# Splitting the next expert's weights into a second pair of tiles, two jobs ahead

## The chip, the core and the metric

The kernel runs on one core of a Trainium2 chip. The metric is the device time of one execution in microseconds (us); where several runs were timed, their median is given. The core's engines are TensorE (PE in the profile, with its weight loads as PEld), VectorE (DVE), ScalarE (ACT), GpSimd (POOL) and SyncE (SP, which here issues DMAs). Each has its own queue of instructions and waits for the others through semaphores. "PEq", "DVEq" or "ACTq" in a row of the trace is the sequencer of that engine: its branches, register operations and waiting steps.

## The reference, cut to what matters

Two stages follow each other. The first is a recurrence over 768 positions for 4 batches and 8 heads; its output is the list of 3072 tokens with 384 channels that the second takes.

```python
for t in range(S):
    cur = einsum('bhd,bhe->bhde', u * k[t], v[t])
    y[t] = einsum('bhd,bhde->bhe', r[t], state + cur)
    state = w * state + einsum('bhd,bhe->bhde', k[t], v[t])

logits = x @ w_gate + modality_bias[modality_id]
e_idx  = argmax(logits);  gate_w = softmax(logits) at e_idx
for e in range(8):
    h = maximum(x[e_idx == e] @ w1[e], 0)       # 384 -> 1024
    out[e_idx == e] = gate_w * (h @ w2[e])      # 1024 -> 384
```

Each token goes to one expert only. With the inputs timed here, three of the eight experts have tokens: 149, 1354 and 1569. The expert with 1569 comes first, that with 149 last.

## The kernel before, in words

**Tiling.** The recurrence is worked in chunks with matrix products (the first stage, up to about 225 us), during which finished tokens are routed and ten portions of 128 tokens of the first expert are already put through its weights (the "slots"). What is left is cut into **jobs** of 128 tokens of one expert. Job 0 stands ahead of a loop, jobs 1 to 15 are turns of it (`For_i`, L1441). Jobs 0 to 2 belong to the first expert that has tokens, 3 to 13 to the second, 14 and 15 to the third.

**Weights.** w1 and w2 of one expert are 6144 fp32 numbers in each partition, `raw`; the first half of the columns is w1, the second w2. For the products they are scaled by a power of two (`ws`) and split into two fp16 tiles: ScalarE writes `whi`, the rounded value, and VectorE `wlo`, what the rounding left (`split`, L954, in pieces of WQ = 1024 columns, six of them). The scale comes from a norm of each piece, taken on ScalarE (`norm`, L916) and summed and turned into `ws` and its inverse `winv` by `scales`. `wf` is the product of the two inverses and belongs to the output's factor; `undo` (L937) renews it. There is one `raw`, one `whi` and one `wlo`, so the weights of the next expert can be loaded while those in use are in `whi` and `wlo`, but not split.

**A job.** On TensorE: the last products of the job before (`low_terms`, from its `hl`), then `up`: the hidden blocks in three groups of 4, 2 and 2 (`phb`, nine terms a block from `whi` and `wlo`), then `high_terms` of this job (`po`, from `hh`). After each group ScalarE evicts it to `hh` (`relu_high`, L1010) and VectorE writes the remainder to `hl` (`relu_low`, L1015). ScalarE also scales the output row of the job before (`otb`, L966, by `fac`), which GpSimd scatters by an indirect DMA. At the end `take_in` (L1398) copies the next tokens, which have landed in `xn` and `mn`, to `mxT` and `mt`, where the next job's products read them.

**What runs in which job.** A table with a column for each job is worked out on VectorE once the tokens are counted (`jobs`, L862 to L888; TensorE then spreads it, L891). Its row CODE holds a small number with bits, which each turn loads into registers of the engines concerned (`at`, L898). Run-time branches (`tc.If`) on that number decide what a turn does. Below, a branch is called *taken* where its body runs and *passed* where it doesn't:

- `first_half` (L1408), at the end of the last job of an expert: the split of w1 into `whi` and `wlo`, once TensorE is through with the old w1.
- `second_half` (L1413), at the start of the first job of an expert: `undo` and the split of w2, with part of the last piece on GpSimd, after the old w2 has been used by `low_terms`.
- otherwise, in the Else of `second_half`, two inner branches (L1430 and L1432), each with three norms of the weights that were loaded since: the first three in the expert's last job but one, the others in its last.

SyncE loads the weights of the expert after next in the first job of an expert (`next_load`, L1435), as soon as `raw` has been read.

**What sets the order.** The first stage and job 0 are one block whose instructions are put in the order of the code on each engine (`manual_schedule`, closed at L1402), but the branch of `first_half` for job 0 (L1440) stands outside of it, as a whole; so does the loop. Within the loop's body, four engines run in the order of the code. At run time, each engine works through its own queue in order.

Of the kernel before, what the change touches and what calls it, by code (L numbers as in the profile page):

```python
# [18 lines left out]
P = 128  # L19
# [16 lines left out]
GONE = 1000  # L36
NQ = 6
# [19 lines left out]
SP, ACT, AD = (mybir.EngineType.SP,), (mybir.EngineType.Activation,), (mybir.EngineType.Activation, mybir.EngineType.DVE, mybir.EngineType.Pool)  # L57
# [3 lines left out]
class _Kernel:  # L61
# [730 lines left out]
    def jobs(self):  # L792
# [62 lines left out]
        eq = new("eq", [P, 4, E])  # L855
        v.scalar_tensor_tensor(eq, csm.unsqueeze(1).to_broadcast([P, 4, E]), self.line, self.grid, ALU.subtract, ALU.is_equal)
# [5 lines left out]
        f, g = new("jf", [P, 4]), new("jg", [P, 4])  # L862
# [5 lines left out]

        last, now, soon, then = (slice(q, q + 1) for q in range(4))
        a, b = new("ja", [P, 1]), new("jbit", [P, 1])
        v.tensor_scalar(a, f[:, now], -1.0, 1.0, ALU.mult, ALU.add)
        v.scalar_tensor_tensor(b, f[:, last], 2.0, g[:, soon], ALU.add, ALU.mult)
        yield
        v.scalar_tensor_tensor(b, g[:, then], a, b, ALU.mult, ALU.add)
# [67 lines left out]
    def wide(self, q, part=0, parts=1, n=1):  # L944

        sl, sc = self.piece(q, part, parts, n)
        self.nc.scalar.activation(self.whi[:, sl], self.raw[:, sl], AF.Copy, scale=sc)

    def fine(self, q, part=0, parts=1):

        sl, sc = self.piece(q, part, parts)
        self.nc.vector.scalar_tensor_tensor(self.wlo[:, sl], self.raw[:, sl], sc, self.whi[:, sl], ALU.mult, ALU.subtract)  # L952

    def split(self, q, parts=1):  # L954
# [138 lines left out]
    def run(self):  # L1093
# [313 lines left out]
        whole = self.late.tile([P, 768], F32, name="scaled")  # L1407
        def first_half(code):  # L1408
            with tc.If(code > 7):
                for q in range(NQ // 2):  # L1410
                    self.split(q, 2 if q == 0 else 1)

        def second_half(code):  # L1413
            with tc.If(code % 8 > 3) as first:
                self.undo()
                self.split(NQ // 2)

                sl, sc = self.piece(NQ - 1, 0, 1)
                lo, hi = slice(sl.stop - 768, sl.stop), slice(sl.stop - 512, sl.stop)
                nc.gpsimd.tensor_tensor(whole, self.raw[:, lo], sc.to_broadcast([P, 768]), ALU.mult)  # L1420
                nc.gpsimd.tensor_tensor(self.whi[:, hi], self.raw[:, hi], sc.to_broadcast([P, 512]), ALU.mult)
                mid = slice(sl.start - WQ, hi.start)
                nc.scalar.activation(self.whi[:, mid], self.raw[:, mid], AF.Copy, scale=sc)
                self.fine(NQ - 2)
                rest = slice(sl.start, lo.start)
                nc.vector.scalar_tensor_tensor(self.wlo[:, rest], self.raw[:, rest], sc, self.whi[:, rest], ALU.mult, ALU.subtract)
                nc.gpsimd.tensor_tensor(self.wlo[:, lo], whole, self.whi[:, lo], ALU.subtract)
            with first.Else():
                with tc.If(code % 4 > 0):
                    with tc.If(code % 2 > 0):  # L1430
                        norms(*range(NQ // 2))
                    with tc.If(code % 4 > 1):  # L1432
                        norms(*range(NQ // 2, NQ))
# [6 lines left out]
        first_half(self.at(CODE, 0, 15, AD))  # L1440
        with tc.For_i(1, nj, 1, iteration_sync="reg_based") as i, tc.manual_schedule(engines={getattr(mybir.EngineType, e) for e in MS[:4]}):  # L1441
            self.turn(0, self.at(ROW, i, E * CAP, SP, 1), mn, xn)
            code = self.at(CODE, i, 15, AD)
            self.low_terms(po)
            second_half(code)
# [7 lines left out]
            first_half(code)  # L1453
# [45 lines left out]
```

## Time and profile before

| | |
|---|---|
| three timed runs | 368.51, 368.72, 372.12 us; median 368.72 |
| the profiled execution | 372.59 us, of it a span of 370.9 us between its first and last instruction |
| mean granted TensorE clock | 0.962 of full speed |
| busy: TensorE / its weight loads | 339.8 / 270.4 us |
| busy: VectorE / ScalarE / GpSimd | 230.5 / 157.5 / 175.0 us |
| instructions | 14643 |

Rows of the timeline read: start in us from the span's start, length of the stretch, engine, line, operation, output <- inputs, shape of output and input, number of instructions in it, and in brackets how long the engine stood idle just ahead and what released it. Rows of the windows give a stretch of time, its length, and each engine's busy time in it with the number of instructions; then the granted clock, the DMA share and GB/s. A row of one line's instructions on a sequencer gives their count, three lengths in ns, and the first and the last start.

### The profile page before, as it was taken

How to read it: one execution, taken by the hardware profiler on the slowest of the kernel's cores; microseconds unless marked ns; L12 is line 12 of the kernel's file. 1: busy time of each engine (PE TensorE's matmuls, PEld its weight loads, DVE VectorE, ACT ScalarE, POOL GpSimd, SP SyncE). 2: the span in 40 equal slices, each digit the busy share in tenths (PEclk: the TensorE clock that was granted, in tenths of full speed). 3: DMA queues.
4: the chain of work that ended last, by engine and by line, in shares of the span. 5: the costliest groups of instructions: out<-in, count | busy, mean ns of one | idle time of the engine just before them, and what ended most of it. 6: DMA issues, size and time to landing. Idle time of an engine off the chain costs nothing. (4 is left out here: it accounts for less than half of the span.)

```text
span 370.9 us, 14643 instructions
## 1 busy us (share of the span) xinstructions
PE 339.8 (92%) x5314; PEld 270.4 (73%) x5314; DVE 230.5 (62%) x754; ACT 157.5 (42%) x371; POOL 175.0 (47%) x252
## 2 busy tenths in 40 slices
PE   7969999898989999999989599998899999999883
PEld 3658888688777978878867487776677788767661
DVE  6996767679979596679755444339533233323960
ACT  7135647534356455646723122227122222265711
POOL 8974656846985778565241711116111112102821
PEclk9986999989998998999989989999999999999999
DMA  6997796569999998966691412213931211212120
GB/s 158 263 221 217 233 264 175 169 149 171 207 272 172 195 257 208 169 190 164 200 184 31 150 23 51 58 43 86 292 73 43 60 46 43 64 21 64 21 55 4
DMA packets 56091, 50.66 MB, mean 137 GB/s; under 512 B 40936, under 2 KB 49641, under 8 KB 55792
## 3 DMA queue, kind: packets, MB, share of 16 engines
q1 hardware_dynamic: 52848, 40.60, 49.4%
q0 software_dynamic: 3200, 9.47, 7.4%
q8 instruction: 30, 0.49, 0.6%
q14 instruction: 13, 0.11, 0.1%
HBM read 30.55 MB, written 11.63 MB: 114 GB/s over the span
## 5 line engine op out<-in xcount | busy, mean ns | idle before, releaser
L1006 PEld LDWEIGHTS <-whi 128*128 128x128 f16 x1248 | 73.7, 98 | 8.9 <-issue 6.2
L1080 PEld LDWEIGHTS <-hh 128*128 128x128 f16 x416 | 38.4, 98 | 30.7 <-ACT hh L1010 5.5
L1006 PE MATMUL phb<-mxT,whi 128*128 128x128 f16 x720 | 47.7, 219 | 0.2 <-DVE mt L1398 0.2
L1006 PEld LDWEIGHTS <-wlo 128*128 128x128 f16 x624 | 38.9, 100 | 3.1 <-DVE wlo L952 3.1
L1010 ACT ACTIVATE hh<-phb 128x256 f16<-128x256 f32 (+1 forms) x45 | 20.2, 453 | 42.4 <-PE po L1080 16.6
L1006 PE MATMUL phs<-mxT,whi 128*128 128x128 f16 x480 | 32.1, 223 | 5.0 <-issue 5.0
L1015 DVE SCALAR_TENSOR_TENSOR hl<-phb,hh 128x256 f16<-128x256 f32 (+1 forms) x45 | 22.8, 512 | 20.7 <-ACT hh L1010 13.7
L345 POOL TENSOR_TENSOR rc<-ud,powr 128x512 f32<-128x512 f32 (+1 forms) x27 | 32.8, 1221 | 0.9 <-DVE w L150 0.9
L648 POOL DMA_INDIRECT rows<-row,posi x24 | 24.3, 1013 | 17.0 <-issue 9.7
L425 DVE TENSOR_TENSOR at<-psc,mask 128x512 f32<-128x512 f32 x48 | 31.6, 682 | 0.8 <-PE psc L419 0.7
L454 PE MATMUL py<-kv,at 128*64 128x48 f32 x768 | 30.9, 236 | 1.2 <-issue 1.2
L454 PEld LDWEIGHTS py<-kv,at 128*64 128x64 f32 x768 | 29.1, 152 | 2.6 <-issue 1.8
L1085 PEld LDWEIGHTS <-hl 128*128 128x128 f16 x208 | 19.6, 98 | 15.6 <-issue 3.5
L419 PE MATMUL psc<-rc,kc 48*64 48x128 f32 x768 | 28.7, 284 | 2.2 <-issue 1.4
L1006 PE MATMUL phb<-mxT,wlo 128*128 128x128 f16 x360 | 28.0, 219 | 2.6 <-DVE wlo L952 2.6
L362 POOL TENSOR_TENSOR rk<-rc,kc 128x512 f32<-128x512 f32 x14 | 17.8, 1274 | 26.1 <-DVE ebx L299 12.2
L530 ACT ACTIVATE row<-py,sx 128x384 f16<-128x384 f32 x24 | 13.9, 579 | 34.3 <-DVE sx L301 19.7
L1090 DVE TENSOR_SCALAR fac<-mt,wf 128x1 f32<-128x1 f32 x16 | 3.4, 213 | 40.2 <-ACT otb L966 32.2
L1080 PE MATMUL po<-wlo,hh 128*128 128x384 f16 x128 | 26.3, 326 | 2.0 <-DVE wlo L952 2.0
L1080 PE MATMUL po<-whi,hh 128*128 128x384 f16 x128 | 26.8, 327 | 0.6 <-ACT hh L1010 0.6
L975 POOL TENSOR_TENSOR seenb<-otb,putb 128x1 int32<-128x1 int32 x15 | 2.8, 188 | 51.0 <-ACT otb L966 48.2
L419 PEld LDWEIGHTS psc<-rc,kc 48*64 48x64 f32 x768 | 21.7, 136 | 6.0 <-issue 3.1
(268 smaller groups left out, 690.7 us busy)
## 6 DMA issues: line engine op xcount, KB each, us to landing
ud<-in_pd SPq DMA_DIRECT2D x48, 192.0 KB
kv<-in_pt SPq DMA_DIRECT2D x24, 384.0 KB
raw<-in_w SPq DMA_DIRECT2D x12, 512.0 KB
raw<-in_w SPq DMA_DIRECT2D x2, 1536.0 KB, 7.7
r<-in_pt SPq DMA_DIRECT2D x10, 192.0 KB
rows<-pad SPq DMA_DIRECT2D x1, 1544.0 KB
rows<-row,posi POOLq DMA_INDIRECT x24, 4.2
xn<-rows SPq DMA_TRANSPOSE x16
```

The costliest lines, as they stand in the source:

```text
L345: nc.gpsimd.tensor_mul(u["rc"][:, s], u["rT"][:, s], self.powr[:, s])
L362: nc.gpsimd.tensor_mul(u["rk"], u["rc"], u["kc"])
L419: nc.tensor.matmul(u["ps"][j][s, pr * P : (pr + 1) * P], u["kc"][r, pr, s], u["rc"][r, pr, :], start=True, stop=True)
L425: nc.vector.tensor_mul(u["at"][:, j * NPR : (j + 1) * NPR, :], u["ps"][j].rearrange("p (q t) -> p q t", q=NPR), self.mask.unsqueeze(1).to_ ...
L454: nc.tensor.matmul(py[t, sl], u["at"][:, j * NPR + pr, t], u["v"][:, sl], start=c == h == 0, stop=h == H - 1 and i >= BARE, skip_group_che ...
L530: self.nc.scalar.activation(u["x16"][:, :DM], u["x"], AF.Copy, scale=u["g"]["sx"][:, b : b + 1])
L648: i = nc.gpsimd.indirect_dma_start(out=self.rows, out_offset=bass.IndirectOffsetOnAxis(ap=u["posi"][:, b : b + 1], axis=0), in_=u["row"][: ...
L1006: self.nc.tensor.matmul(ph[:, q * P : (q + 1) * P], w[:, c0 : c0 + P], self.xT[:, xq, t * P : (t + 1) * P], start=i == q == 0, stop=i == l ...
L1010: self.nc.scalar.activation(self.hh[:, f0 : f0 + fb, t * P : (t + 1) * P], p3, AF.Relu)
L1015: self.nc.vector.scalar_tensor_tensor(self.hl[:, f0 : f0 + fb, r], p3, 0.0, self.hh[:, f0 : f0 + fb, r], ALU.max, ALU.subtract)
L1080: self.nc.tensor.matmul(po[:, :DM], self.hh[:, f, t * P : (t + 1) * P], w[:, c0 : c0 + DM], start=n == q == f == 0, stop=False)
L1085: self.nc.tensor.matmul(po[:, :DM], self.hl[:, f, t * P : (t + 1) * P], self.whi[:, c0 : c0 + DM], start=False, stop=f == FB - 1)
```

## The change

The table gets seven positions ahead and behind an expert's first job in place of four (`OFFS`), and CODE six bits in place of four. GpSimd no longer loads the code. A second pair of fp16 tiles, `nhi` and `nlo`, each of the size of `whi`, is made in the pool "late", which takes the memory that the first stage has given back. The steps of a change of expert, counted from the first job of the new one:

| job | step | bit |
|---|---|---|
| 5 ahead, 4 ahead | norms of w1 and of w2 | 2 and 4 |
| 3 ahead, at the end | `staged(0)`: w1 is split into `nhi`, `nlo` | 8 |
| 2 ahead, at the end | `staged(1)`: the same for w2 | 16 |
| 1 ahead, at the end | `moved(0)`: w1 is copied from `nhi`, `nlo` to `whi`, `wlo` | 32 |
| the first, after `low_terms` | `undo` and `moved(1)`: the same for w2 | 1 |

Each `moved` is four fp16 copies of 1536 columns, three on VectorE and one on ScalarE. All but the last row of the table are now called from `next_of`, at the end of the job: an outer branch (any bit above the lowest), and in it five branches one after the other. For the first change of expert the norms have been taken in the first stage, as before.

```diff
-SP, ACT, AD = ..., (mybir.EngineType.Activation, mybir.EngineType.DVE, mybir.EngineType.Pool)
+SP, ACT, AD = ..., (mybir.EngineType.Activation, mybir.EngineType.DVE)
...
-        last, now, soon, then = (slice(q, q + 1) for q in range(4))
...
-        v.scalar_tensor_tensor(field[:, CODE : CODE + 1], f[:, soon], 8.0, b, ALU.mult, ALU.add)
+        v.scalar_tensor_tensor(code, col(f, 1), 2.0, s2, ALU.mult, ALU.add)
+        yield
+        for bit in (s1, n2, n1, col(f, 0)):
+            v.scalar_tensor_tensor(code, code, 2.0, bit, ALU.mult, ALU.add)
+            yield
...
-        whole = self.late.tile([P, 768], F32, name="scaled")
-        def first_half(code):
-            with tc.If(code > 7):
-                for q in range(NQ // 2):
-                    self.split(q, 2 if q == 0 else 1)
-
-        def second_half(code):
-            with tc.If(code % 8 > 3) as first:
...
+        nhi, nlo = (self.late.tile([P, 2 * WC], F16, name=n, bufs=1) for n in ("nhi", "nlo"))
+        half = [slice(q * WC // 2, (q + 1) * WC // 2) for q in range(4)]
+
+        def moved(q):
+            for to, of in ((self.whi, nhi), (self.wlo, nlo)):
+                nc.vector.tensor_copy(to[:, half[2 * q]], of[:, half[2 * q]])
+            nc.vector.tensor_copy(self.whi[:, half[2 * q + 1]], nhi[:, half[2 * q + 1]])
+            nc.scalar.copy(self.wlo[:, half[2 * q + 1]], nlo[:, half[2 * q + 1]])
+
+        def first_of(code):
+            with tc.If(code % 2 > 0):
                 self.undo()
...
-            with first.Else():
-                with tc.If(code % 4 > 0):
-                    with tc.If(code % 2 > 0):
-                        norms(*range(NQ // 2))
-                    with tc.If(code % 4 > 1):
-                        norms(*range(NQ // 2, NQ))
+                moved(1)
+
+        def staged(q):
+            for q in range(q * NQ // 2, (q + 1) * NQ // 2):
+                self.split(q, 1, nhi, nlo)
+
+        def next_of(code):
+            with tc.If(code > 1):
+                for bit, f in ((2, lambda: norms(*range(NQ // 2))), (4, lambda: norms(*range(NQ // 2, NQ))), (8, lambda: staged(0)), (16, lambda: staged(1)), (32, lambda: moved(0))):
+                    with tc.If(code % (2 * bit) > bit - 1):
+                        f()
...
-        first_half(self.at(CODE, 0, 15, AD))
+        next_of(self.at(CODE, 0, 63, AD))
...
-            second_half(code)
+            first_of(code)
...
             self.high_terms(po)
-            first_half(code)
+            next_of(code)
```

Three places show how the instructions move. ScalarE, around the branch for job 0, ahead of the loop, before (`pha0` to `pha2` are the three groups of job 0; L1409 is the branch of `first_half`):

```order
L1010 ACTIVATE hh_288<-pha0_4480 128x4x128
L1010 ACTIVATE hh_288<-pha1_4527 128x2x128
L900 TENSOR_LOAD tab_4443
L1409 COMPARE_AND_BRANCH
L947 ACTIVATE whi_291<-raw_290,ws_294 128x512 x2
L947 ACTIVATE whi_291<-raw_290,ws_294 128x1024 x2
L1409 UNCONDITIONAL_BRANCH x2
L1010 ACTIVATE hh_288<-pha2_4548 128x2x128
```

and now, from the body of the branch on bit 8, which is the one taken in job 0 (L1435 are the five branches, L1433 the outer one, L963 the split):

```order
L963 ACTIVATE nhi_4616<-raw_290,ws_294 128x1024 x3
L1435 UNCONDITIONAL_BRANCH x2
L1435 COMPARE_AND_BRANCH
L1421 COPY wlo_292<-nlo_4617 128x1536
L1435 UNCONDITIONAL_BRANCH x2
L1435 REGISTER_ALU
L1435 COMPARE_AND_BRANCH
L963 ACTIVATE nhi_4616<-raw_290,ws_294 128x1024 x3
L1435 UNCONDITIONAL_BRANCH x2
L1433 UNCONDITIONAL_BRANCH
L1017 ACTIVATE hh_288<-pha2_4564 128x2x128
```

In both, the whole branch stands between the evictions of the second and the third group of job 0. In job 0 the branch of before isn't taken; of the new ones, the outer and that on bit 8 are.

VectorE, at the end of a turn of the loop, before:

```order
L1015 SCALAR_TENSOR_TENSOR hl<-phb_4775,hh 128x2x128
L1398 COPY mxT<-xn 128x6x128
L1398 COPY mt_300<-mn 128x4
L1409 COMPARE_AND_BRANCH
L952 REGISTER_ALU
L952 SCALAR_TENSOR_TENSOR wlo<-raw,ws,whi 128x512
```

and now (L1405 is `take_in`):

```order
L1405 COPY mxT<-xn 128x6x128
L1405 COPY mt_300<-mn 128x4
L1433 COMPARE_AND_BRANCH
L1435 REGISTER_ALU
L1435 COMPARE_AND_BRANCH
L1435 UNCONDITIONAL_BRANCH x2
L1435 REGISTER_ALU
L1435 COMPARE_AND_BRANCH
L1435 UNCONDITIONAL_BRANCH x2
L1435 REGISTER_ALU
L1435 COMPARE_AND_BRANCH
L964 REGISTER_ALU
L964 SCALAR_TENSOR_TENSOR nlo<-raw,ws,nhi 128x1024
```

Ahead of the first subtraction of a half stood one branch; now the outer one and, for w1, three of the five stand there, the two on the norms being empty on VectorE.

VectorE, the table's last steps ahead of `jd`, which TensorE multiplies (L891 of before, L905 now), before:

```order
L866 SCALAR_TENSOR_TENSOR field<-jr,linep,field 128x1
L873 TENSOR_SCALAR ja<-jf 128x1
L874 SCALAR_TENSOR_TENSOR jbit<-jf,jg 128x1
L876 SCALAR_TENSOR_TENSOR jbit<-jg,ja,jbit 128x1
L878 TENSOR_TENSOR mr<-eq,nx 128x7
L880 SCALAR_TENSOR_TENSOR jbit<-jf,jbit 128x1
L881 TENSOR_REDUCE field<-mr 128x1
L883 SCALAR_TENSOR_TENSOR field<-jf,jbit 128x1
L888 TENSOR_TENSOR jd<-field,id_143 40x160
L1015 SCALAR_TENSOR_TENSOR hl<-phs_1_4370,hh 128x4x128
```

and the end of it now:

```order
L891 TENSOR_TENSOR jbits<-jbits,jg 128x1
L892 TENSOR_TENSOR jbits<-jbits,jg 128x1
L894 SCALAR_TENSOR_TENSOR field<-jf,jbits 128x1
L1022 SCALAR_TENSOR_TENSOR hl<-phs_1_4370,hh 128x4x128
L1072 TENSOR_SCALAR fac<-mt_299,wf 128x1
L1073 TENSOR_TENSOR ids<-mt_299,skip 128x1
L897 SCALAR_TENSOR_TENSOR field<-field,jbits 128x1 x3
L897 SCALAR_TENSOR_TENSOR field<-field,jf 128x1
L902 TENSOR_TENSOR jd<-field,id_143 40x160
```

`jd` stood ahead of the last remainder of slot 9 and of its factor; now four steps of the code and `jd` stand behind them.

More of the change, by code (lines that the diff above doesn't have):

```diff
@@ L36 @@
 GONE = 1000
+OFFS = 7
 NQ = 6
@@ L56 @@
 ROW, CODE, MORE, SEEN = range(4)
-SP, ACT, AD = (mybir.EngineType.SP,), (mybir.EngineType.Activation,), (mybir.EngineType.Activation, mybir.EngineType.DVE, mybir.EngineType.Pool)
+SP, ACT, AD = (mybir.EngineType.SP,), (mybir.EngineType.Activation,), (mybir.EngineType.Activation, mybir.EngineType.DVE)
 WQ = 2 * WC // NQ
@@ L854, in jobs @@
         v.reduce_sum(jr, od, axis=AX.X)
-        eq = new("eq", [P, 4, E])
-        v.scalar_tensor_tensor(eq, csm.unsqueeze(1).to_broadcast([P, 4, E]), self.line, self.grid, ALU.subtract, ALU.is_equal)
+        eq = new("eq", [P, OFFS, E])
+        v.scalar_tensor_tensor(eq, csm.unsqueeze(1).to_broadcast([P, OFFS, E]), self.line, self.grid, ALU.subtract, ALU.is_equal)
         yield
@@ L861, in jobs @@
         v.scalar_tensor_tensor(nx[:, : E - 1], eid[:, 1:], float(E), act[:, 1:E], ALU.add, ALU.mult)
-        f, g = new("jf", [P, 4]), new("jg", [P, 4])
+        f, g = new("jf", [P, OFFS]), new("jg", [P, OFFS])
         v.reduce_sum(f, eq[:, :, 1:], axis=AX.X)
@@ L866, in jobs @@
         v.scalar_tensor_tensor(field[:, SEEN : SEEN + 1], jr[:, 0:1], self.linep, field[:, ROW : ROW + 1], ALU.add, ALU.subtract)
-        last, now, soon, then = (slice(q, q + 1) for q in range(4))
-        a, b = new("ja", [P, 1]), new("jbit", [P, 1])
-        v.tensor_scalar(a, f[:, now], -1.0, 1.0, ALU.mult, ALU.add)
-        v.scalar_tensor_tensor(b, f[:, last], 2.0, g[:, soon], ALU.add, ALU.mult)
+        col = lambda x, q: x[:, q + 1 : q + 2]
+        go, a, b, bits = new("jgo", [P, 1]), new("ja", [P, 1]), new("jb2", [P, 1]), new("jbits", [P, 4])
+        n1, n2, s1, s2 = (bits[:, q : q + 1] for q in range(4))
+        v.tensor_scalar(go, col(f, 0), -1.0, 1.0, ALU.mult, ALU.add)
+        v.scalar_tensor_tensor(a, self.line, 0.0, col(f, -1), ALU.is_equal, ALU.max)
         yield
-        v.scalar_tensor_tensor(b, g[:, then], a, b, ALU.mult, ALU.add)
+        v.tensor_tensor(n2, col(g, 2), col(g, 3), ALU.max)
+        v.tensor_tensor(b, col(f, 1), col(f, 2), ALU.max)
+        v.tensor_mul(s2, col(f, 2), go)
         mr = new("mr", [P, E - 1])
@@ L879, in jobs @@
         yield
-        v.scalar_tensor_tensor(b, f[:, now], 4.0, b, ALU.mult, ALU.add)
+        v.tensor_tensor(n1, n2, col(g, 4), ALU.max)
+        v.tensor_mul(b, b, a)
+        v.tensor_mul(a, a, col(f, 1))
+        v.tensor_mul(s1, col(f, 3), go)
+        yield
+        v.tensor_mul(bits[:, 0:2], bits[:, 0:2], col(f, 0).to_broadcast([P, 2]))
+        v.tensor_max(s2, s2, a)
+        v.tensor_max(s1, s1, b)
         v.reduce_sum(field[:, MORE : MORE + 1], mr, axis=AX.X)
         yield
-        v.scalar_tensor_tensor(field[:, CODE : CODE + 1], f[:, soon], 8.0, b, ALU.mult, ALU.add)
+        v.tensor_max(n1, n1, col(g, 5))
+        v.tensor_max(n2, n2, col(g, 4))
+        code = field[:, CODE : CODE + 1]
+        v.scalar_tensor_tensor(code, col(f, 1), 2.0, s2, ALU.mult, ALU.add)
         yield
+        for bit in (s1, n2, n1, col(f, 0)):
+            v.scalar_tensor_tensor(code, code, 2.0, bit, ALU.mult, ALU.add)
+            yield
         wide = [NJ, 4, NJ]
@@ L942, in piece, with split @@
         return slice(q * WQ + part * w, q * WQ + part * w + n * w), self.ws[:, 2 * q // NQ : 2 * q // NQ + 1]
[L944 to L954, printed above, removed]
+    def split(self, q, parts=1, hi=None, lo=None):
+        hi, lo = (self.whi, self.wlo) if hi is None else (hi, lo)
         for part in range(parts):
-            self.wide(q, part, parts)
-            self.fine(q, part, parts)
+            sl, sc = self.piece(q, part, parts)
+            self.nc.scalar.activation(hi[:, sl], self.raw[:, sl], AF.Copy, scale=sc)
+            self.nc.vector.scalar_tensor_tensor(lo[:, sl], self.raw[:, sl], sc, hi[:, sl], ALU.mult, ALU.subtract)
     def put(self, po, t, key):
```

19 lines of the change are left out of this document (4 added, 15 removed).

## The prediction

> **What bounds it now.** The page comes first, then the stretches between the starts of jobs in the loop, cut where TensorE begins a job's first product (in this order jobs 1, 3, 4, 6, 12 and 14, then two stretches of the first stage).
>
> ```profile
> span 370.9 us, 14643 instructions
> PE 339.8 (92%) x5314; PEld 270.4 (73%) x5314; DVE 230.5 (62%) x754; ACT 157.5 (42%) x371; POOL 175.0 (47%) x252
> ```
>
> ```profile
> core 0: us, PE busy (x) PEld busy (x) DVE busy (x) ACT busy (x) POOL busy (x), PEclk, DMA share, GB/s
> 236.25:244.19 7.94, 7.94 (x98) 6.32 (x97) 2.79 (x11) 1.95 (x4) 1.36 (x3) 1.00 0.07 25
> 252.24:263.38 11.14, 8.61 (x98) 6.19 (x97) 10.87 (x19) 5.36 (x8) 5.36 (x4) 1.00 0.59 183
> 263.38:271.70 8.32, 8.16 (x98) 6.24 (x98) 2.88 (x11) 1.94 (x4) 1.36 (x3) 1.00 0.98 210
> 279.71:287.72 8.01, 8.01 (x99) 6.31 (x97) 2.77 (x11) 1.94 (x4) 1.36 (x3) 1.00 0.20 49
> 328.04:337.03 8.99, 8.29 (x99) 6.40 (x98) 2.58 (x11) 5.80 (x12) 1.35 (x3) 1.00 0.18 45
> 344.97:356.40 11.43, 8.85 (x100) 6.19 (x97) 10.96 (x17) 5.42 (x8) 7.58 (x6) 1.00 0.12 27
> 186.50:188.75 2.25, 1.14 (x19) 1.07 (x19) 1.13 (x2) 0.00 (x0) 1.60 (x4) 1.00 0.73 264
> 188.75:192.16 3.41, 3.41 (x45) 3.10 (x43) 1.28 (x6) 1.43 (x4) 1.81 (x14) 0.50 1.25 160
> ```
>
> TensorE is the bound: an ordinary job (the 8.01 row) is matmul from end to end. Jobs 3 and 14, the first of their experts, take 11.14 and 11.43 us; job 4 takes 8.32 (its tokens land behind the weight load), job 12 takes 8.99 (ScalarE takes the weights' norms). Over 8.01 these come to 3.13 + 0.31 + 0.98 + 3.42 = 7.84 us, the most there is to win. The stops are these, from TensorE's timeline (idle before, and its releaser, in brackets):
>
> ```profile
> 255.25 0.68 PE L1006 MATMUL phb<-mxT,wlo 128*128 128x128 f16 x9 [1.33 <-DVE wlo L952]
> 260.36 0.81 PE L1080 MATMUL po<-wlo,hh 128*128 128x384 f16 x4 [0.71 <-DVE wlo L952]
> 333.12 1.15 PE L1080 MATMUL po<-whi,hh 128*128 128x384 f16 x6 [0.56 <-ACT hh L1010]
> ```
>
> **Part by part.** With first jobs 3 and 14 the new code gives: split of the first half at the end of jobs 0 and 11, of the second at the end of 1 and 12, copies at the end of 2 and 13 and the start of 3 and 14, norms at the end of 9 and 10. Splits and first-half moves now stand in five Ifs in a row, of which a special job takes one and passes four. What an If costs is in the timelines of ScalarE and VectorE, and in the rows of the two inner Ifs of before (L1430, L1432; first and last start):
>
> ```profile
> 327.74 1.06 ACT L917 ACTIVATE junk<-raw 128x1024 f16<-128x1024 f32 x1 [1.88 <-PE po L1085]
> 331.06 0.19 ACT L917 ACTIVATION_READ_ACCUMULATOR junk<-raw 128x1 f32 x1
> 331.99 0.58 ACT L966 ACTIVATE otb<-po,fac 128x384 f32<-128x384 f32 x1 [0.74 <-PE L1006]
> 335.99 1.06 ACT L917 ACTIVATE junk<-raw 128x1024 f16<-128x1024 f32 x1 [2.38 <-PE po L1080]
> 342.46 0.38 ACT L1010 ACTIVATE hh<-phb 128x256 f16<-128x256 f32 x1 [1.45 <-PE L1080]
> 342.76 4.45 ACT L947 ACTIVATE whi<-raw,ws 128x512 f16<-128x512 f32 x5
> ```
> ```profile
> L1430 DVEq ALU_OP  x2: 55/56/57, 328.6 to 337.5; - x2
> L1432 DVEq ALU_OP  x2: 55/56/57, 329.1 to 337.9; - x2
> L966 ACTq EVENT_SEMAPHORE  x4: 17/38/38, 331.7 to 331.9; - x4
> ```
> ```profile
> 350.87 2.48 DVE L952 SCALAR_TENSOR_TENSOR wlo<-raw,ws,whi 128x1024 f16<-128x1024 f32 x2
> 353.67 0.20 DVE L1090 TENSOR_SCALAR fac<-mt,wf 128x1 f32<-128x1 f32 x1
> 356.11 0.16 DVE L1398 COPY mt<-mn 128x4 int16<-128x4 int16 x1
> 358.82 0.21 DVE L1090 TENSOR_SCALAR fac<-mt,wf 128x1 f32<-128x1 f32 x1 [2.54 <-issue]
> 362.59 0.35 DVE L1398 COPY mxT<-xn 128x768 f16<-128x768 f16 x1
> 362.85 0.16 DVE L1398 COPY mt<-mn 128x4 int16<-128x4 int16 x1
> ```
>
> Job 12 takes the first inner If and passes the second, job 13 the other way: ScalarE reaches its norms 1.88 and 2.38 us after its last eviction, so a passed If costs it 0.50. VectorE, which has nothing in either, goes from the one to the next in 0.5 and 0.4; I take 0.45. Behind work that time isn't hidden: after the last norm (331.25) ScalarE stands 0.74 us before the output row, whose sums TensorE had finished by 328.04. Taken Ifs are nearly free: the split at 342.76 follows the eviction of 342.46 at once. A wait step is 0.07 (four from 331.7 to 331.9). [...]
>
> VectorE first. From `fac` to the last copy it works 2.60 us without a stop (353.67 to 356.27), and the way round the loop to the next `fac` is 2.54: 5.14 of 8.01. A staging job adds three subtractions (2.48 / 2 each, 3.7), four passed Ifs (1.8), entry and exit (0.3, estimated) and the waits (0.4); it loses one passed If of before (0.45), and about 0.4 runs beside the last copies: 10.5 us, 2.5 more than TensorE's job. Where it also waits for ScalarE's first piece (three passed Ifs, waits and 1.1 us after an eviction at 5.4) it is 11.2. The move of the first half can't begin before the last copy of its job, 6.6 us into an ordinary one (363.01 against 356.40): four Ifs, waits and one copy of 1536 columns (0.6, estimated from 0.35 for 768) put the first weights 2.7 us behind that copy.
>
> So the second expert's first job starts 6.6 + 11.2 + 2.7 = 20.5 us after job 1 did, in place of 16.0: **4.5 lost**. Moves of the second half and ScalarE's copies lie beside the first product and cost nothing; without that cover they would be 1.5.
>
> Norms, jobs 9 and 10: they no longer stand behind the loop's turn, but pass three Ifs more and one less on the way to the output row, so that comes 1.0 to 1.5 us later than in job 12 of before, which lost 0.98: job 10 loses about **2.2**, and VectorE is 0.8 late into job 11. From there the chain is 6.6 + 0.8 + 10.5 + 10.5 + 2.7 = 31.1 in place of 24.0: **7.1**. Loop: 4.5 + 2.2 + 7.1 - 7.84 = +6.0. Bounds for these Ifs: 0, as where taken, or 0.6, with all the 0.74 put down to one.
>
> Ahead of the loop, job 0's staging stands, on ScalarE and VectorE both, before the eviction of that job's last two blocks:
>
> ```profile
> 232.55 0.38 ACT L1010 ACTIVATE hh<-pha 128x256 f16<-128x256 f32 x1 [0.56 <-PE pha L1006]
> 234.30 0.49 PE L1080 MATMUL po<-whi,hh 128*128 128x384 f16 x2
> ```
>
> Those blocks are waited for at 234.30, and their low part, then the next tokens' copy, before 236.25. Now: two Ifs and waits from 232.55 to 233.6, first piece 234.75, subtractions to 238.5, two Ifs, eviction and copy to 240.1: **+3.9**. With Ifs at nothing it is 1.9.
>
> The table's arithmetic: nine more small instructions ahead of `jd`, four of them behind an eviction.
>
> ```profile
> 223.04 0.21 DVE L866 SCALAR_TENSOR_TENSOR field<-jr,linep,field 128x1 f32<-128x1 f32 x1
> 224.06 0.32 DVE L888 TENSOR_TENSOR jd<-field,id 40x160 f32<-40x160 f32 x1
> 226.52 0.54 PE L891 MATMUL ptab<-jd,ones 40*128 40x160 f32 x2
> ```
>
> Eight took 1.02 us; seventeen take 2.1 to 225.1, then eviction and meta 0.9, four dependent ones 0.8 and `jd` 0.3: 227.1 against 226.52, **+0.6**, for TensorE waits in order. Gone at no gain: GpSimd's three products, and its slowing of VectorE. The weight load goes out 2 us sooner, behind job 3's tokens as before.
>
> The sum is 6.0 + 3.9 + 0.6 = +10.5 on the profiled execution (372.59, of it 370.9 span). The median shown is 368.72, 1% under that; the microseconds carry over: 379.2.
>
> **Rivals.** Cheap control: the sequencer runs ahead, as at 342.76, and passed Ifs hide. Then job 0 costs 1.9, the table 0.6, the tight VectorE cycles (5.1 + 3.7 + 0.4) about 3 over both changes, and 7.84 goes: -2.3 to -4, 365.5 with the wait on ScalarE and 364.5 without. Against it: the 0.74 idle, and 2.38 against 1.88. [...] 0.13.
>
> Half-price Ifs, partly behind copies: chains of 18.2 and 26.8 us, norms 1.0, so 2.2 + 2.8 + 1.0 - 7.84 = -1.8; with 2.9 and 0.6 ahead of the loop +1.7: 370.4, no change that can be told. 0.14.
>
> Clock: TensorE was granted half speed from 188.75 to 192.16, right after 2.25 us of which it worked 1.14; in job 3 of before, idle 1.33 us, it was not. Job 0's stop of 3.5 us and job 14's of about 3 may each bring such a window, at 1.7 us: 382.6. [...] 0.15.
>
> That staging falls on other jobs is ruled out by the two jobs in which before splits.
>
> **The numbers.** Forecast 0.58. What a measurement here can tell from no change is about 1%, 365.0 to 372.4. Faster 0.13 (the first rival), same 0.11 (most of the second), slower 0.76 (the forecast, the clock and the rest of the second). Range: from 370.4, the half price, to 387: Ifs at 0.6 add some 4.5 us over both chains, norms and job 0, and the clock 3.4.
>
> **What would show it.** In the changed profile: VectorE's cycle from last copy to last copy 10 to 11 us in jobs 1, 2, 12 and 13 with idle stretches released by no one ahead of `nlo` and `fac`; TensorE waiting for VectorE's `whi` copy at the start of jobs 3 and 14, 2.5 to 3 us each; for ScalarE's `hh` in job 10 some 2 us; in job 0 3.5 us ahead of its last four products. Wrong: ordinary lengths there, or stops that name the copies of the second half.

## The result

The changed kernel takes 390.5 us (median of five runs, 388.8 to 392.6) against 368.7 us: **1.057 times the kernel before, 95% interval 1.052 to 1.063**. Slower was forecast, but by 10.5 us, and 390.5 lies above the range, which ended at 387. The profiled execution took 391.9 us, of it a span of 390.0. All ratios below are of fast runs alone, and the traces are of such runs too, except that of `e3_both` (384.5 us, against 376.4 to 381.7 in its other three runs).

The page of the changed kernel, span and busy times:

```profile
span 390.0 us, 14559 instructions
PE 345.8 (89%) x5314; PEld 274.0 (70%) x5314; DVE 228.8 (59%) x778; ACT 164.5 (42%) x375; POOL 161.7 (41%) x245
```

TensorE runs as many products as before and is busy 6.0 us longer with them; the rest of the loss is idle time. The stretches between the first products of jobs show both (columns as in the prediction; in this order jobs 0, 1, 2, 3, 4, 9, 10, 11, 12, 13, 14, and 15 with what follows it):

```profile
226.08:240.14 14.06, 10.13 (x99) 6.75 (x97) 5.94 (x12) 5.17 (x7) 1.36 (x3) 0.80 0.24 44
240.14:253.55 13.41, 8.64 (x98) 6.83 (x97) 6.34 (x14) 5.17 (x7) 1.36 (x3) 0.88 0.14 30
253.55:264.23 10.68, 10.37 (x97) 8.56 (x98) 3.25 (x13) 2.99 (x5) 1.36 (x3) 0.78 0.14 37
264.23:272.19 7.96, 7.96 (x98) 6.41 (x98) 4.99 (x17) 3.64 (x6) 1.18 (x2) 1.00 0.84 320
272.19:280.42 8.23, 8.12 (x99) 6.39 (x98) 2.45 (x11) 1.73 (x4) 1.54 (x4) 1.00 0.47 131
312.53:321.26 8.73, 8.21 (x99) 6.21 (x96) 2.64 (x11) 4.68 (x9) 1.37 (x3) 1.00 0.26 58
321.26:330.67 9.41, 8.29 (x98) 6.32 (x98) 2.45 (x11) 5.45 (x11) 1.36 (x3) 1.00 0.14 37
330.67:343.07 12.40, 8.29 (x97) 6.32 (x98) 6.12 (x14) 5.29 (x10) 1.37 (x3) 1.00 0.20 42
343.07:356.90 13.83, 9.75 (x97) 7.93 (x97) 6.23 (x14) 5.17 (x7) 1.36 (x3) 0.88 0.11 29
356.90:366.99 10.09, 9.75 (x98) 7.95 (x98) 3.17 (x13) 3.00 (x5) 1.36 (x3) 0.83 0.15 39
366.99:374.94 7.95, 7.95 (x97) 6.40 (x98) 4.98 (x17) 3.63 (x6) 1.36 (x3) 1.00 0.05 14
374.94:390.00 15.06, 8.34 (x99) 6.14 (x96) 2.64 (x11) 2.53 (x5) 2.54 (x5) 0.93 0.12 28
```

Jobs 3 and 14, which took 11.14 and 11.43 us before, are ordinary now: the change does what it says there. What it costs is in the jobs ahead of them: 2.1 us in jobs 9 and 10, and the rest in jobs 0, 1, 2, 11, 12 and 13. In five of the last six the granted clock is under 1.00, and TensorE is busy for 8.6 to 10.4 us with work that takes 8.0 in an ordinary job. TensorE's timeline names the stops:

```profile
235.57 0.82 PE L1087 MATMUL po<-whi,hh 128*128 128x384 f16 x2 [3.34 <-ACT hh L1017]
237.63 2.72 PE L1092 MATMUL po<-whi,hl 128*128 128x384 f16 x8 [0.59 <-DVE mxT L1405]
253.55 2.74 PE L1013 MATMUL phb<-mxT,whi 128*128 128x128 f16 x24 [4.77 <-DVEq L1435]
264.23 1.51 PE L1013 MATMUL phb<-mxT,whi 128*128 128x128 f16 x24 [0.31 <-DVE whi L1419]
326.58 1.15 PE L1087 MATMUL po<-whi,hh 128*128 128x384 f16 x6 [1.10 <-ACT hh L1017]
343.07 2.25 PE L1013 MATMUL phb<-mxT,whi 128*128 128x128 f16 x24 [3.89 <-DVEq L1435]
356.90 2.41 PE L1013 MATMUL phb<-mxT,whi 128*128 128x128 f16 x24 [4.09 <-DVEq L1435]
366.99 1.51 PE L1013 MATMUL phb<-mxT,whi 128*128 128x128 f16 x24 [0.34 <-DVE whi L1419]
```

The three large stops of the loop come ahead of the first products of jobs 2, 12 and 13, and they were released by VectorE's sequencer on L1435, the five branches (below, the *ladder*), not by a copy or an eviction. The waits for moved weights, 2.5 to 3 us in the forecast, are 0.31 us in job 3 and 0.34 in job 14. The move itself takes what was forecast: VectorE's last copy in job 2 ended at 261.55 (`mt`, from 261.39), and the first moved weights are there 2.63 us later, where the forecast had 2.7:

```profile
263.62 0.56 DVE L1419 COPY whi<-nhi 128x1536 f16<-128x1536 f16 x1 [2.07 <-DVEq L1435]
```

But TensorE, held at the start of job 2 and then at half clock, is late itself (job 2 takes 10.68 us), so little of that is left to wait for.

What VectorE's sequencer did on that line ahead of job 2, and who waited for it, is in the rows of L1435 for 246 to 254 us (count, lengths in ns, first and last start; then idle us and times of the engines that waited), with VectorE's own work in that time behind them:

```profile
L1435 DVEq EVENT_SEMAPHORE  x2: 21/21/21, 247.9 to 253.5; - x2
  PE phb L1013: 4.8, 1
```
```profile
246.91 0.16 DVE L1405 COPY mt<-mn 128x4 int16<-128x4 int16 x1
249.76 3.67 DVE L964 SCALAR_TENSOR_TENSOR nlo<-raw,ws,nhi 128x1024 f16<-128x1024 f32 x3 [2.69 <-ACT nhi L963]
255.44 0.21 DVE L1097 TENSOR_SCALAR fac<-mt,wf 128x1 f32<-128x1 f32 x1 [2.00 <-DVEq L1424]
```

The next tokens were in place at 247.1. TensorE starts job 2 at 253.55, straight after the waiting step that the sequencer ends its ladder with, at 253.5, and that step comes after the last subtraction (249.76 + 3.67 = 253.43). The last branch of the ladder is the one on bit 32, the move of w1, which writes `whi` and `wlo`. Job 1 passes it, but TensorE's first product reads `whi`, and whether it has been rewritten is known only once VectorE is past that branch. This reading is the first theory, **the gate**: the unneeded branch on bit 32 stands behind the staging, and so the staging, which TensorE doesn't need, holds TensorE up.

### The profile page after: what moved, and what is told of

Read it like the earlier page. It is cut to its first block, busy times and chain, and to the rows that moved or that the text cites. A ratio compares the mean times of both kernels' runs of the same rounds, so it can differ in the third digit from the quotient of the medians.

```text
span 390.0 us, 14559 instructions
## 1 busy us (share of the span) xinstructions
PE 345.8 (89%) x5314; PEld 274.0 (70%) x5314; DVE 228.8 (59%) x778; ACT 164.5 (42%) x375; POOL 161.7 (41%) x245
## 5 line engine op out<-in xcount | busy, mean ns | idle before, releaser
L1013 PEld LDWEIGHTS <-whi 128*128 128x128 f16 x1248 | 77.0, 102 | 24.8 <-DVEq L1435 15.2
L1013 PE MATMUL phb<-mxT,whi 128*128 128x128 f16 x720 | 51.9, 230 | 13.9 <-DVEq L1435 13.3
L1013 PEld LDWEIGHTS <-wlo 128*128 128x128 f16 x624 | 40.8, 103 | 0.2 <-issue 0.2
L420 PE MATMUL psc<-rc,kc 48*64 48x128 f32 x768 | 31.6, 289 | 3.4 <-DVE settled L745 1.9
L455 PE MATMUL py<-kv,at 128*64 128x48 f32 x768 | 28.7, 226 | 1.1 <-issue 1.1
L420 PEld LDWEIGHTS psc<-rc,kc 48*64 48x64 f32 x768 | 23.5, 140 | 8.5 <-issue 5.6
L1013 PE MATMUL phb<-mxT,wlo 128*128 128x128 f16 x360 | 29.4, 228 | 0.0
L455 PEld LDWEIGHTS py<-kv,at 128*64 128x64 f32 x768 | 26.6, 142 | 2.2 <-issue 1.9
```

Source lines behind the costliest of these rows:

```text
L420: nc.tensor.matmul(u["ps"][j][s, pr * P : (pr + 1) * P], u["kc"][r, pr, s], u["rc"][r, pr, :], start=True, stop=True)
L455: nc.tensor.matmul(py[t, sl], u["at"][:, j * NPR + pr, t], u["v"][:, sl], start=c == h == 0, stop=h == H - 1 and i >= BARE, skip_group_che ...
L1013: self.nc.tensor.matmul(ph[:, q * P : (q + 1) * P], w[:, c0 : c0 + P], self.xT[:, xq, t * P : (t + 1) * P], start=i == q == 0, stop=i == l ...
```

## The experiments

Theory A is the gate; theory B, the rival, is the prediction's own picture carried on: the staging takes that much time on in-order engines and holds everything behind it, wherever the branches stand. Where ratios are given they are to the kernel before, run in turns on the same chip; `e4` to `e6` were timed in a session in which the kernel before is faster as well (356.7 us, against 368 to 371 in the others). The length of the first stage differs from execution to execution by several us (in the traces of the other kernels job 0 begins between 223 and 230 us). So traces are also compared from job 0's first product to the end of the span:

| | before | changed | e1 | e2 | e3 | e7 | e8 | e9 |
|---|---|---|---|---|---|---|---|---|
| job 0's first product to the end, us | 142.6 | 163.9 | 148.2 | 165.1 | 148.7 | 151.7 | 142.4 | 141.8 |

For `e9` this leaves out what its staging, moved into the first stage, may cost there. In `e1`, `e3` to `e6`, `e8` and `e9` the move of w1 stands ahead of its staging. With these inputs each bit falls on a job of its own, so nothing is left out; for an expert of a single job both would fall into one, and the order would have to be the other. These kernels are experiments, then, and not replacements.

### The branch on bit 32 first

```diff
-for bit, f in ((2, ...), (4, ...), (8, ... staged(0)), (16, ... staged(1)), (32, ... moved(0))):
+for bit, f in ((32, ... moved(0)), (2, ...), (4, ...), (8, ... staged(0)), (16, ... staged(1))):
```

> The changed kernel with one thing moved: in the ladder of five branches the one on bit 32 (the move of w1) stands first instead of last. Theory A (gate): TensorE's first product of every job reads a tile that the move of w1 may write, so it waits until VectorE has passed that branch, and VectorE reaches it only behind the staging. Then the stops of 4.77, 3.89 and 4.09 us ahead of the first products of jobs 2, 12 and 13 shrink to under 1 us each, the stretches of half clock right behind them go (1.7 us each), and what is left is what the prediction had worked out, VectorE's late evictions and copies: 1 to 3 us in each of jobs 2, 3, 12, 13 and 14. Time 379 us (376 to 382). Theory B (engine time): the staging itself, 3.7 us of VectorE and its branches, holds TensorE through everything that stands behind it on VectorE, wherever the branch stands: stops of the same size come up inside the same jobs, time 388 to 391.

Measured: 375.3 us, ratio 1.017 (1.007 to 1.027): the first place in the ladder instead of the last is worth about 4% of the kernel before, 15 us. The stops of the loop in this kernel, from TensorE's timeline (all over 0.6 us from job 1 to job 14):

```profile
252.40 1.14 PE L1087 MATMUL po<-whi,hh 128*128 128x384 f16 x6 [1.30 <-DVEq L1424]
269.19 1.15 PE L1087 MATMUL po<-whi,hh 128*128 128x384 f16 x6 [0.74 <-ACT hh L1017]
319.30 1.15 PE L1087 MATMUL po<-whi,hh 128*128 128x384 f16 x6 [1.80 <-ACT hh L1017]
337.29 1.14 PE L1087 MATMUL po<-whi,hh 128*128 128x384 f16 x6 [1.27 <-ACTq L1435]
346.10 1.14 PE L1087 MATMUL po<-whi,hh 128*128 128x384 f16 x6 [0.71 <-DVEq L1424]
```

The stops ahead of the first products of jobs 2, 12 and 13 are gone, and no stretch of half clock begins in the loop. Theory A holds, and B falls. But the time is below A's 376 to 382 too. VectorE's timeline says why:

```profile
245.29 0.16 DVE L1405 COPY mt<-mn 128x4 int16<-128x4 int16 x1
248.57 3.68 DVE L964 SCALAR_TENSOR_TENSOR nlo<-raw,ws,nhi 128x1024 f16<-128x1024 f32 x3 [3.11 <-SPq L1440]
252.62 0.21 DVE L1097 TENSOR_SCALAR fac<-mt,wf 128x1 f32<-128x1 f32 x1 [0.38 <-ACT hh L1017]
254.94 0.16 DVE L1405 COPY mt<-mn 128x4 int16<-128x4 int16 x1
255.01 0.55 DVE L1419 COPY whi<-nhi 128x1536 f16<-128x1536 f16 x1
```

`fac` follows the last subtraction after 0.38 us; in the changed kernel it took 2.00. Behind the staging there is now no passed branch, and by these 0.38 us the sequencer goes round the loop while VectorE still subtracts. The move follows the last copy at once (254.94, then 255.01): with its branch first, the four passed branches that made up most of the 2.7 us (in the changed kernel their waiting steps are at 262.3 and 262.9) no longer stand ahead of it. VectorE's cycle in job 2, last copy to last copy, is 9.65 us (245.29 to 254.94), not 10.5 to 11.2. A passed branch behind work can cost more than its own steps: on the ladder of the changed kernel the last compare ahead of job 2 is at 251.9, but the waiting step that ends the branch on bit 32 is at 253.5, when the subtractions have ended (253.43).

### Job 0's ladder behind its evictions, without and with the first edit

```diff
-        ms.close()
-        self.ordered = False
         self.actx.close()
...
         next_of(self.at(CODE, 0, 63, AD))
+        ms.close()
+        self.ordered = False
```

With that, job 0's ladder stands in the order of the code: behind the eviction of the third group and behind `take_in`.

> The changed kernel with job 0's ladder behind the eviction of that job's third group and the copy of the next tokens instead of ahead of them; order of the branches as in the changed kernel. Theory A (gate): the stop of 3.34 us in job 0 goes, but TensorE then waits ahead of job 1's first product for VectorE to pass the branch on bit 32 behind the same staging, 3 to 4.5 us, with its stretch of half clock; 388 to 391, no change. Theory B (the order in job 0 has its own price): the stop of 3.34 + 0.59 us and 2.5 us of half clock go and nothing takes their place; 384.

> Both edits: the branch on bit 32 first in the ladder, and job 0's ladder behind that job's last evictions and copies. Theory A (gate): the two work together; job 0's 3.9 us of stops and 2.5 us of half clock go as well, and 0.5 to 2 us come back in job 1 as late evictions: 374 us (371 to 376), more than the two edits save apart. Theory B: 381 to 384, the saving of the second edit alone.

Measured: `e2_job0` 392.1 us, 1.058 (1.047 to 1.069), no better than the changed kernel, as A had it; `e3_both` 380.6 us, 1.025 (1.013 to 1.036), where A had 371 to 376. The interval of `e3_both` overlaps that of `e1_move_first` (1.007 to 1.027), and from job 0's first product on they take 148.7 and 148.2 us, so the edit of job 0 brought nothing in either. TensorE's timeline of `e2_job0` shows where the stop of job 0 went:

```profile
237.63 2.72 PE L1092 MATMUL po<-whi,hl 128*128 128x384 f16 x8 [4.80 <-DVEq L1444]
254.07 2.72 PE L1013 MATMUL phb<-mxT,whi 128*128 128x128 f16 x24 [4.95 <-DVEq L1433]
```

The stop of 3.34 us is now one of 4.80 ahead of the first product in the loop, released by VectorE's sequencer on L1444, the loop's own line (in `e3_both` the same, 4.73). So A was right on `e2_job0` by another mechanism than it named, and wrong on `e3_both`: at its entry the loop is a second gate, at which TensorE waited 4.80 and 4.73 us until VectorE had come that far.

### The branch on bit 32 between the two stagings

```diff
-(8, ... staged(0)), (16, ... staged(1)), (32, ... moved(0))
+(8, ... staged(0)), (32, ... moved(0)), (16, ... staged(1))
```

> The changed kernel with the branch on bit 32 between the two stagings: order 2, 4, 8, 32, 16. Theory A (TensorE's first product waits for VectorE to pass the branch on bit 32): the staging of w2 (bit 16), at the end of jobs 1 and 12, now stands behind it, so the stops ahead of jobs 2 and 13 (4.77 and 4.09 us) and the half clock behind them go, with 1 to 1.5 us of late evictions in their place; the staging of w1 (bit 8), at the end of job 11, still stands ahead of it, so the stop ahead of job 12 stays at 3.9 (3.5 to 4.3) with its half clock. About 11 us less than the changed kernel: 1.03 of the kernel before. Theory B (what waits is not tied to that branch): the three stops go or stay together.

Measured: 378.4 us, 1.028 (1.023 to 1.034). TensorE's timeline at jobs 2, 12 and 13:

```profile
252.19 1.14 PE L1087 MATMUL po<-whi,hh 128*128 128x384 f16 x6 [1.33 <-DVEq L1424]
335.45 1.51 PE L1013 MATMUL phb<-mxT,whi 128*128 128x128 f16 x24 [3.18 <-DVEq L1435]
348.85 1.14 PE L1087 MATMUL po<-whi,hh 128*128 128x384 f16 x6 [1.24 <-ACT hh L1017]
```

Just the stop that A named stays, ahead of job 12's first product; jobs 2 and 13 have late evictions of 1.33 and 1.24 us instead. This settles the gate. The stop that stays, 3.18 us, is a little under the expected 3.5, and no half clock follows it (1.51 us for the 24 products).

### What is left: job 0, and late evictions

Three kernels on top of `e1_move_first`. `e4_job0_early` puts job 0's branches for norms and staging ahead of that job's first eviction:

```diff
-        self.up("a", lambda: next(once, lambda: None)())
+        self.scales("1")
...
+        next_of(code, (2, 4, 8, 16))
+        self.up("a")
...
+        with tc.If(code > 31):
+            moved(0)
         ms.close()
```

> The kernel with the branch on bit 32 first, and in addition job 0's scale and its branches for norms and staging ahead of job 0's first eviction instead of ahead of its third; the branch on bit 32 for job 0 stands behind its last copy. Where ScalarE and VectorE are free at the start of job 0 the staging should be hidden there, and TensorE meets no waiting engine at the entry of the loop. Theory A (the 6.1 us that job 0 lost is a matter of where the staging stands): the stops of 3.4 and 1.1 us shrink to about 1.5 together and the half clock behind them goes; job 0 takes 9.5 us instead of 14.0; 371 us (369 to 373), or 4.5 us under the kernel it is made from. Theory B (the staging's time counts wherever it stands ahead of the loop): job 0 stays at 13 to 14 us and the time at 375.

`e5_norms_act` gives the norms branches of their own, on ScalarE alone (`own` is the code loaded by ScalarE only), and `e6_all` has both edits:

```diff
+            with tc.If(code > 7):
+                ... (32, moved(0)), (8, staged(0)), (16, staged(1))
+            with tc.If(own % 8 > 1):
+                ... (2, norms), (4, norms)
```

> The kernel with the branch on bit 32 first, and in addition the two branches on the norms on ScalarE alone, by a second register, in an outer branch of their own behind the others: VectorE passes two branches fewer on its way to each staging and out of it, and ScalarE two or three fewer. Theory A (the price of passed branches is what is left): 0.4 to 0.5 us each, so the stops in jobs 2, 11, 12 and 13 (1.30, 0.48, 1.27 and 0.71 us) shrink by 0.5 to 0.8 each and that of job 10 (1.80) by about 0.9; 3 us under the kernel it is made from, 372. Theory B (passed branches are hidden, the staging's own work is what is left): stops as they were, 375.

> All three edits together. Theory A: job 0 takes 9 to 10 us and the stops of the loop sum to about 4 instead of 7; 368 us (366 to 370), 2 us under the kernel before, no difference that can be told from it or just one. Theory B: the price of the second job's staging stays, 371 to 375, slower than before.

Measured: 1.010 (1.005 to 1.014), 1.010 (1.005 to 1.014) and 1.008 (1.004 to 1.012). TensorE's stops in job 0 of `e4_job0_early`, and in jobs 2, 10, 12 and 13 of `e5_norms_act`:

```profile
217.89 1.71 PE L1087 MATMUL po<-whi,hh 128*128 128x384 f16 x6 [2.53 <-ACT hh L1017]
```
```profile
239.33 1.15 PE L1087 MATMUL po<-whi,hh 128*128 128x384 f16 x6 [1.26 <-ACT hh L1017]
304.80 1.15 PE L1087 MATMUL po<-whi,hh 128*128 128x384 f16 x6 [0.58 <-ACT hh L1017]
322.44 1.15 PE L1087 MATMUL po<-whi,hh 128*128 128x384 f16 x6 [1.57 <-ACT hh L1017]
331.16 1.15 PE L1087 MATMUL po<-whi,hh 128*128 128x384 f16 x6 [0.60 <-ACT hh L1017]
```

In `e4_job0_early` job 0's stops shrink to 2.53 us and the one at the loop's entry is gone, but half clock follows (1.71 us for six products of 1.15), and job 0 takes 12.3 us instead of the 9.5 of theory A. In `e5_norms_act` the norms' stop in job 10 falls from 1.80 to 0.58 us, as expected for two or three passed branches fewer on ScalarE. The staging's stops don't: 1.26, 1.57 and 0.60 against 1.30, 1.27 and 0.71, though VectorE passes two branches fewer. They wait for `hh` from ScalarE. So passed branches on VectorE alone are not what is left. But `e5` does not show that passed branches cost nothing. ScalarE, too, passes two fewer ahead of the staging, and begins it 1.46 us after its last eviction instead of 2.52; the branch for the norms, though, now stands behind the staging. These are the output rows of job 2 that follow the staging, in `e1_move_first` and then in `e5_norms_act`:

```profile
250.99 0.58 ACT L973 ACTIVATE otb<-po,fac 128x384 f32<-128x384 f32 x1 [0.58 <-PE phb L1013]
238.21 0.58 ACT L973 ACTIVATE otb<-po,fac 128x384 f32<-128x384 f32 x1 [2.61 <-PE phb L1013]
```

What was won ahead of the staging, 1.06 us, is lost again behind it, 2.03. In time, `e4_job0_early` and `e5_norms_act` lie where their theories A had them, and `e6_all`, still slower than the kernel before, where its theory B had it; but the intervals of all three overlap that of `e1_move_first`, so the times alone decide nothing here. The next kernel goes for ScalarE.

`e8_apart` has all three edits, and the engines' branches apart: the move is four copies on VectorE in a branch ahead of all others; ScalarE's ladder starts with its half of the staging.

```diff
+        def move_of(dc):                  # dc: the code, on VectorE alone
+            with tc.If(dc > 31):
+                moved(0)
+        def next_of(dc, ac):              # ac: on ScalarE alone
+            with tc.If(ac > 1):
+                ... staged, the nhi part; norms
+            with tc.If(dc % 32 > 7):
+                ... staged, the nlo part
```

> All three edits of before, and the two engines' branches apart: the move is VectorE's alone (four copies in place of three and one), in a branch ahead of all others; ScalarE's ladder holds its half of the staging first and then the norms, VectorE's the subtractions; at the start of a turn ScalarE has no branch any more. Theory A (late evictions come from ScalarE's passed branches ahead of its half of the staging): ScalarE begins its half 1 to 1.5 us sooner, and the stops in jobs 2, 12, 13 and 14 (1.57, 1.75, 0.77, 0.40 us over an ordinary job) fall to 0.5 or less each, job 0 to about 10: 3 to 4 us less than with the three edits alone, 0.5% to 1% under the kernel before. Theory B (the staging's own 3.2 us on ScalarE and 3.7 on VectorE don't fit between two jobs' evictions): jobs 2 and 12 keep 1 us or more each, and the time stays 0.3% to 0.8% above the kernel before.

Measured: 369.0 us, 0.999 (0.996 to 1.003). ScalarE's staging at the end of job 1 and the output row that follows it, and TensorE's stops in jobs 2 and 12:

```profile
240.61 3.23 ACT L1423 ACTIVATE nhi<-raw,ws 128x1024 f16<-128x1024 f32 x3 [1.30 <-DVEq L1428]
245.45 0.58 ACT L974 ACTIVATE otb<-po,fac 128x384 f32<-128x384 f32 x1 [1.61 <-PE phb L1014]
```
```profile
246.57 1.15 PE L1088 MATMUL po<-whi,hh 128*128 128x384 f16 x6 [1.04 <-ACT hh L1018]
329.26 1.14 PE L1088 MATMUL po<-whi,hh 128*128 128x384 f16 x6 [1.62 <-DVEq L1415]
```

Both theories have a part: the stop in job 13 is down to 0.16 us, but jobs 2 and 12 keep 1.04 and 1.62, as B expected. ScalarE begins 1.30 us after its last eviction, released by VectorE's sequencer on L1428, the passed branch of the move, which reads `nhi`: a gate again, this time for ScalarE. It then stages for 3.23 us, and after 1.61 more comes to the row and the eviction that TensorE waits for. B's reason, that the staging doesn't fit between two jobs' evictions, is not shown by this. The branch for the norms still stands behind ScalarE's staging, and 1.61 us is 1.03 more than the 0.58 of `e1_move_first`, where the staging of w2 ends the ladder; that is as much as the stop of 1.04 that stays. A kernel with the engines' branches apart and ScalarE's staging last was not run, so what the staging alone costs stays open. Jobs 1 to 14 together take 4.0 us less than before (116.1 for 120.1), but job 0 takes 10.6 us instead of 8.0, and job 15 with the end 15.8 instead of 14.5: that cancels. Of the last 1.3 us, 0.9 are TensorE's stop at the loop's exit (1.76 us, 0.84 before); why it grew is not shown.

`e9_job0_before_row` moves job 0's staging once more, ahead of the last slot's output row:

> The kernel with the engines' branches apart, and job 0's staging moved once more: ahead of the last slot's output row on ScalarE (which stood ahead of it and waited 3.1 us for TensorE), with the scale taken one slot sooner. Theory A (the 2.48 us left in job 0 are ScalarE's staging standing behind a row that waits for TensorE): the stop shrinks to 0.5 or less, job 0 takes 8 to 8.5 us instead of 10.6, the loop is as it was: 2.2 us less, 0.6% under the kernel before (0.3% to 1.0%). Theory B (the table comes too late for it): job 0 stays at 10 us or more and the time at that of the kernel before.

Measured: 369.4 us, 0.999 (0.996 to 1.003); job 0 takes 9.66 us, with one stop of 1.57. Less than half of the expected 2.2 us came. The rows of the table's last step on VectorE and of ScalarE's staging say why:

```profile
222.19 0.27 DVE L908 CAST tab<-ptab 1x120 int32<-1x120 f32 x1 [0.72 <-PE ptab L906]
```
```profile
223.92 3.23 ACT L1419 ACTIVATE nhi<-raw,ws 128x1024 f16<-128x1024 f32 x3 [4.42 <-issue]
```

The code that the branches read is written at 222.5, and ScalarE, idle by then, begins at 223.9; while the decision comes from that table, at most some 1.5 us could still be won there. So with the gates ahead of TensorE's products removed, the change is worth nothing that can be measured here. No version of it that was run beats the kernel before.

## Why the prediction was wrong

By its own steps; the measured column is from the stretches above, against ordinary jobs of 8.01 us, and for the table from TensorE's timeline, where the products that spread it (224.30 us) have no idle time ahead:

| step | forecast, us | measured, us |
|---|---|---|
| the table's arithmetic | +0.6 | 0: TensorE has no stop ahead of `ptab` |
| job 0 | +3.9 | +6.1 (14.06 for 7.95): stops of 3.34 and 0.59, then half clock |
| first change, job 1 to job 3's start | +4.5 | +8.1 (13.41 + 10.68 for 16.0) |
| norms, jobs 9 and 10 | +2.2 | +2.1 (8.73 + 9.41) |
| second change, job 11 to job 14's start | +7.1 | +12.3 (12.40 + 13.83 + 10.09 for 24.0) |
| what goes | -7.84 | -7.7: jobs 3, 4 and 14 take 7.96, 8.23 and 7.95 |
| after job 15's first product | 0 | +0.6 |
| sum | +10.5 | +21.4 |

From job 0's first product to the end the traces differ by 21.3 us, so the list is complete. The first stage happened to be 2.2 us shorter in the profiled execution of the changed kernel.

**The step that failed** is the chain through VectorE. "VectorE first" let TensorE run on while the staging made VectorE late, and let the lateness come up as missing weights at jobs 3 and 14. It named ScalarE's and VectorE's users of each branch, but never asked what TensorE must know before it may read `whi`: whether the branch on bit 32, the last of the five and behind the staging, has rewritten it. `e1_move_first` and `e7_move_between` show that. The sum of the stops came near all the same: 4.77 + 3.89 + 4.09 + 0.31 + 0.34 = 13.4 us at both changes, against 11.6. That agreement is by chance, for without the gate the chain is much cheaper than forecast: `e1_move_first` loses 1.7% (0.7% to 2.7%), not 2.8%, since the sequencer goes round the loop beside the last subtraction (`fac` 0.38 us behind it, not 2.00).

**The other part that failed** is a rival's size. Half clock was given 0.15 and 3.4 us, for job 0's stop and job 14's. There were four stops of 3.3 us or more, three of them by the gate, and half clock followed each:

```profile
251.49:258.32 6.83, 4.77 (x45) 4.77 (x46) 2.23 (x4) 1.24 (x3) 1.36 (x3) 0.50 0.08 29
343.59:347.00 3.41, 3.41 (x36) 3.41 (x34) 0.28 (x2) 0.26 (x2) 1.18 (x2) 0.51 0.15 58
```

These are two of the four stretches in the windows' view, at the stops of 4.77 and 3.89 us: 6.83 and 3.41 us at a granted clock of one half. Busy time over 8.1 us in jobs 0, 1, 2, 12 and 13 adds up to 2.0 + 0.5 + 2.3 + 1.65 + 1.65 = 8.1 us, which is most of what lies between the forecast of +10.5 and the 21.8 of the medians; the rest is the larger stops. With the gate taken out, the loop's half clock goes too.

**What was right.** Slower, at 0.76. Job 0's stops, 3.34 and 0.59 us against 3.9, by the mechanism that was named: the order of ScalarE's rows around the third eviction. The norms, 2.1 against 2.2, though not in the places that were forecast: of this, 0.53 us is a gate's stop ahead of job 10, and the stop for `hh` in job 10 is 1.10, not 2; without the gate (`e1_move_first`) it is 1.80, and `e5_norms_act` confirms that it is branches on ScalarE. The move's price, 2.63 against 2.7. The first rival, cheap branches and a gain of 2 to 4 us, is refuted for this order of branches. Its mechanism, a sequencer that runs ahead, is what `e1_move_first` shows behind taken branches (`fac` 0.38 us behind the last subtraction). The price of a passed branch on VectorE, 0.45, was near too, for branches with no work for VectorE in them: the compares of two that follow each other start 0.4 us apart.

```profile
L1435 DVEq COMPARE_BRANCH  x2: 119/119/119, 247.0 to 247.4; - x2
```

Two small terms of VectorE's staging cycle, 0.4 us of waits and 0.3 of entry and exit, are shown by no run as they stand. The changed kernel's trace has four waiting steps of 0.05 us on VectorE ahead of the first subtraction (L964; in job 0 from 231.3 to 231.6), seven on ScalarE ahead of its first piece (L963; at the end of job 1 from 247.8 to 248.3), and 0.3 us from the outer branch's compare to the first inner one (L1433 at 246.3, L1435 at 246.6); the exit is not told apart in it.

## What to carry to other kernels

In the kernels here, a run-time branch that may write a tile is a point that TensorE, which reads that tile, waits for, taken or not (in the changed kernel 0.31 us ahead of job 3, where it is taken, and 4.77 ahead of job 2, where it is passed behind the staging): put such a branch ahead of long work that the reader doesn't need (15 us in `e1_move_first`), or on an engine of its own, which was not run, and do the same with the entry of a loop (4.80 us in `e2_job0`). Behind long work, a passed branch can also make its engine run dry (`fac` came 2.00 us after the last subtraction, and 0.38 without it), so work that should overlap with what comes next stands last in its ladder. And before weights are staged ahead, look for the free time between two jobs' evictions on each engine, not for its idle time per job: here ScalarE idles for 6 of 8 us (in an ordinary job of before it is busy for 1.94 of 8.01), and still 3.2 us of staging in one piece, with the branches around it, made evictions late (stops of 1.04 and 1.62 us in `e8_apart`).

## What the runs showed of the hardware that was not expected

- **A passed branch can be a barrier for its own engine.** Where the body that was passed over held work for the engine, the branch ended with a waiting step, and that step came when the engine's earlier work had just ended: in the changed kernel at 253.5 us, behind a subtraction that ended at 253.43; in `e1_move_first` at 245.5, behind a copy that ended at 245.45; on ScalarE in the changed kernel at 251.6, behind a staging that ended at 251.61. Of the four branches that VectorE passes at the end of job 1 in the changed kernel, those for the norms, which hold nothing for it, have no such step. Behind the same subtractions without a passed branch, the next turn's `fac` came after 0.38 us instead of 2.00.
- **Half clock began and ended on a grid of 3.41 us, and did not go by the length of a stop alone.** In the changed kernel's trace all edges of half clock from job 0 to job 14 (234.42, 241.25, 251.49, 258.32, 343.65, 347.06, 357.30 and 360.71 us) lie whole multiples of 3.41 us apart. Each trace is cut here into windows along its own edges. From job 0's first product to the last product, in the eleven traces, all 13 full-clock windows in which TensorE was busy for at most 1.23 us were followed by half clock (four of them in the changed kernel, busy for 1.23, 0.71, 0.58 and 0.40 us), and none with 1.46 us or more. So half clock followed all eleven stops of 3.34 to 4.95 us, but not the one of 3.18 us in `e7_move_between`, which an edge cuts in two (1.99 and 1.65 us busy). Of four stops of 2.5 to 2.6 us in job 0 it followed the two that lay in one window (`e4_job0_early` and `e5_norms_act`, 0.88 and 0.81 us busy), and not the two that an edge cuts (`e6_all`, `e8_apart`). No run shifted a stop against the grid on purpose, and in the first stage the limit is less sharp (a window with 1.89 us, 183.22 to 186.63, was followed by half clock in the changed kernel, one with 1.91 in `e2_job0` was not).
